# Attention scores in plain float32, a head's keys split over the two halves of the array's rows

## The chip, the cores and the metric

One program runs on 1 core of a Trainium2 chip. The core has five engines with their own instruction streams: TensorE (PE, with its weight loads as PEld), VectorE (DVE), ScalarE (ACT), GpSimd (POOL) and SyncE (SP), which here issues the DMAs. The metric is device time in microseconds, the median of several runs. A profile is one execution; its span is what the trace covers, and its own time is a little longer.

## The reference

Three blocks in a row. B = 2, H = 8 heads, S = 576 positions, D = 64 per head; hidden width of the bias network 32.

```python
scores = scale * q @ k.T                         # per batch and head, 576 x 576, scale = 1/8
x = log1p(|i - j|) / log1p(max(i, 1))            # one number per pair of positions
bias = relu(x * w1 + b1) @ w2                    # 32 hidden, one bias per head
attn = softmax(scores + bias);  out = attn @ v
# 1152 tokens x 512: four dense experts (512 -> 1024 -> 512), weighted by normalised domain_probs
out += p[:, e] * (relu(x @ w1[e]) @ w2[e])
# second model: (x @ w_a) * (x @ w_b) @ w_out, width 1536
```

All arithmetic is float32. The second model's weights arrive as float64 and are converted in the kernel.

## The kernel before, in words

**Numbers.** TensorE works on rounded float32 ("fp32r", one pass). To keep float32 accuracy a value x is split into hi = round(x) and lo = x - hi, and products are made of three or four such parts. Some small products (bias, attention times values, transposes) run in plain float32 instead, which TensorE does in several passes; the trace then shows two instructions per matmul.

**Order.** The kernel writes a list of operations with engines, durations, buffers and a rank (`op`, rank from RANK); `Plan.run` plays them through a small model and issues each engine's instructions in the order that comes out. A free engine takes the ready operation with the lowest rank; ties go by the time since when it is ready (BY_AGE) and then by its place in the program. Where ENGINES names two engines, the one with the earlier modelled end takes it. Expert matmuls have rank 2 ("fill"), so TensorE takes them when nothing else is ready; with MARGIN an attention matmul waits 300 ns after it became ready while there is fill. A buffer is a tile of a `Room`; operations wait for a tile in the order of the program.

**Attention bias.** 36 groups of 16 positions. Each makes four ramps over the distance (`hh`, L356 on VectorE and L358 on ScalarE), multiplies them by w2 on four column groups of the array (L370, 32 columns each), adds a correction (L388, L390), mirrors one end (L395) and stores its rows to a table in HBM, `bias_d` (L405). A tile of 128 query rows for two heads is loaded back from there (`bt`, L458). Groups 0 to 7 (bias0) serve the first 128 rows, 8 to 15 (bias1) the next, the others (bias2) the rest.

**Scores.** Head pairs m = 0..3, batches b, row tiles t = 0..4 (t = 4 holds 64 rows of both heads). `inputs` (L431 to L444) loads q and k of a pair; `heads` in `_layout` has written each head's 64 dimensions twice, on partitions 0 to 63 and 64 to 127. q becomes a rounded tile and a tile of differences (L440, L441). k is rounded on all partitions (L442), and on the lower 64 the difference takes its place (L443). So a matmul over 128 partitions multiplies q_hi by k_hi and k_lo at once, a second one q_lo, and two column halves of 288 fill two PSUM banks: four matmuls per head and row tile (L490). For the second head of t = 4, whose keys are rotated by 64 columns, there are six, of 288, 224 and 64 columns. There is one staging tile each for q and k (`q2`, `k2`) and two sets of results; two more sets live as guests in x_hi and x_lo for b = 0, m = 2 and 3.

VectorE subtracts the scores from the bias and finds the minimum (L493), ScalarE takes exp and sums (L503), four transposes and a tail bring the weights into key rows (L516, L533 to L536), `values` multiplies by v on two column halves of the array (L581) and normalises into x_hi, x_lo (L587 to L590). Four banks for scores exist at first as two tiles; when seven of the first eight row groups are finished, one of these tiles and two transposing banks go to the experts, so that one score tile is left.

**Experts and second model.** Pass 0 takes the first 256 tokens of batch 0 and starts when their x is finished, amid the rest of attention; pass 1 the others. `up` (L708) and `down` (L719) are matmuls of three parts; weights are loaded (L617) and split (L234, L619). The second model uses a scheme with seven block products, whose sums of inputs are made from transposed token tiles: for the first 256 columns by `x2_first` (L772, transposes L783, then sums from PSUM), for the last 320 by `x2_second` (L815, sums first, then transposes of the tokens and of the sums L842; its third part on 64 rows). The products are L878.

Of the kernel before, what the change touches and what calls it, by code (L numbers as in the profile page):

```python
# [37 lines left out]
RANK = {"prep": 0.5, "bias0": 0, "bias1": 0.6, "bias2": 1, "split": 1, "load": 2, "chain": 0, "fill": 2, "x64": 3, "evac": -0.5, "fin": 0, "pv": 0, "split2": 1.5, "px": 0, "evac2": -0.5, "h2": 0}  # L38
ENGINES = {"kcast": "ACT DVE", "ksub": "POOL DVE", "qcast": "DVE", "qsub": "POOL DVE", "pt": "ACT DVE", "tail": "ACT DVE", "side": "ACT DVE", "mirror": "POOL ACT",
           "whi": "ACT DVE", "wlo": "DVE", "xhi": "DVE", "xlo": "POOL DVE", "rb": "ACT DVE", "rx": "ACT DVE", "s64": "POOL DVE",  # L40
           "wsum": "POOL DVE", "whi2": "ACT", "wlo2": "DVE", "px": "ACT DVE", "xsum": "DVE", "xhi2": "ACT", "xlo2": "DVE", "hmul": "DVE", "hlo": "DVE"}
QUICK, BY_AGE, MARGIN, LATE = 0.9, True, 300, True
# [184 lines left out]
def tile_kernel(ctx, tc, qd, kd, vd, cst, probs, w1r, w2r, war, wbr, wor, out):  # L227
# [47 lines left out]
    R = {z: Room() for z in "w wst h1 h2 u z p q2 q k2 k v bt ptb pr rb xf sums rx hh bst ct sum s64 t64 hl64".split()}  # L275
# [143 lines left out]
    QK, fins, guests = {}, [], []  # L419
# [8 lines left out]

    def inputs(m, b, c):
        w = CW[c]  # L430
        q2, k2 = new("q2"), new("k2")  # L431
        if (b, c) == (0, 0) and m >= 2:
            d = slice(2 * m - 4, 2 * m - 2)
            k = Buf(t=x_hi[:, d, C0:C0 + S])
            q = Buf(t=tuple(x_lo[:, d, C0 + z * C0:2 * C0 + z * C0] for z in range(2)))
        else:
            k, q = new("k"), new("q")
        op({"SP": 440}, lambda e: nc.sync.dma_start(out=q2.t[:, :, :w], in_=qd[m, b][:, :, C0 * c:C0 * c + w]), w=[q2], size=P * 8 * w)
        op({"SP": 440}, lambda e: nc.sync.dma_start(out=k2.t, in_=kd[m, b]), w=[k2], size=P * 8 * S)
        op(t_copy(2 * w, ENGINES["qcast"]), lambda e: copy(e, q.t[0][:, :, :w], q2.t[:, :, :w]), r=[q2], w=[q], prio=RANK["prep"], lock=True)  # L440
        op(t_two(2 * w, ENGINES["qsub"]), lambda e: engine[e].tensor_tensor(out=q.t[1][:, :, :w], in0=q2.t[:, :, :w], in1=f(q.t[0][:, :, :w]), op=ALU.subtract), r=[q2], rw=[q], prio=RANK["prep"], lock=True)  # L441
        op(t_copy(2 * S, ENGINES["kcast"]), lambda e: copy(e, k.t, k2.t), r=[k2], w=[k], prio=RANK["prep"], lock=True)  # L442
        op(t_two(2 * S, ENGINES["ksub"]), lambda e: engine[e].tensor_tensor(out=k.t[D:P], in0=k2.t[D:P], in1=f(k.t[D:P]), op=ALU.subtract), r=[k2], rw=[k], prio=RANK["prep"], lock=True)  # L443
        return q, k  # L444
# [24 lines left out]
    def step(m, b, t, k, q0, Q, K, ptb, sums):  # L469
# [3 lines left out]
        for s in range(2):  # L473
            ps = new("s", "ps")


            r0, r1, c = 0, P, s
            runs = [(half, 0, half * HS, HS) for half in range(2)]
            if t == 4:
                r0, r1, c = ((0, D, 0), (D, P, 0))[s]  # L480
                if s == 1:
                    runs = [(0, 0, D, HS), (1, 0, D + HS, HS - D), (1, HS - D, 0, D)]
            neg = 5 + 2 * k + c

            def qk(e, s=s, ps=ps, runs=runs):
                at = P * t - C0 * (t > 1) + s * CW[1] - D * (t == 4 and s)
                for kk, qz in enumerate(Q.t):
                    lhs = qz[:, s, P * t - C0 * (t > 1):][:, :P] if t < 4 else qz.rearrange("p s w -> p (s w)")[:, at:at + P]
                    for n, (half, o, k0, w) in enumerate(runs):
                        nc.tensor.matmul(ps.t[:, half, o:o + w], lhs, K.t[:, s, k0:k0 + w], start=(kk == 0 and n < 2), stop=(kk == 1 and n in (0, len(runs) - 1)))  # L490
# [15 lines left out]
            if K.room is None:  # L506
                guests.append(o)
# [38 lines left out]
    def values(m, b, ts, w, V, ptb, sums):  # L546
# [42 lines left out]
        op(t_copy(w, ENGINES["xhi"]), lambda e: copy(e, x_hi[:, m, o], xf.t[:, :w]), r=[xf], w=[hi], prio=RANK["fin"], lock=True, after=guests if (b, c) != (0, 0) else ())  # L589
# [169 lines left out]

# [12 lines left out]
    def x2_first(c, i, kind):  # L772
# [41 lines left out]

    def x2_second(c, i, kind):  # L815
        W = DM // 2
        n = P if i < 2 else D
        t0, t1 = (4 * c + i, 4 * c + i + 2 + c) if i < 2 else (6, 6)
        src = [ACC[t0], ACC[t1]]
        if i == 2:  # L820
            far = new("sum")
            op(t_copy(512, ENGINES["px"]), lambda e: copy(e, far.t[0][:D], acc(6)[D:P].rearrange("p (a b) -> p a b", a=2)), r=[ACC[6]], w=[far], prio=RANK["px"])
            a1 = lambda j: far.t[0][:D, j]
            src = [ACC[6], far]
        else:
            a1 = lambda j: acc(t1)[:, W * j:W * j + W]
        sm = new("sum")
        a0 = lambda j: acc(t0)[:n, W * j:W * j + W]
        d = {T1 + j: (lambda j=j: sm.t[j // 2][:n, j % 2]) for j in range(4)}
        got = {}  # L830
        for j, x, y in (T1, lambda: a1(0), lambda: a0(0)), (T2, lambda: a1(1), d[T1]), (T3, lambda: a1(1), lambda: a1(0)), (T4, lambda: a0(1), d[T2]):
            got[j] = op(t_two(W, ENGINES["xsum"]), lambda e, j=j, x=x, y=y: engine[e].tensor_tensor(out=d[j](), in0=x(), in1=y(), op=ALU.subtract), r=src, w=[sm], after={T2: [got.get(T1)], T4: [got.get(T2)]}.get(j, []), prio=RANK["px"], lock=True)
        every = [o for x in ups.values() for o in x] if c else ()
        cols = slice(P * i, P * i + n)
        for j, xs, after in (B11, (lambda: a0(0), lambda: a0(1)), []), (B22, (lambda: a1(1), d[T1]), [got[T1]]), (T4, (d[T4], d[T3]), [got[T4], got[T3]]), (T2, (d[T2],), [got[T2]]):
            u = new(kind, "px")
            k = len(xs)

            def tr(e, u=u, xs=xs):
                for m, x in enumerate(xs):  # L840
                    for h in range(2):
                        nc.tensor.transpose(u.t[:, (2 * m + h) * P:(2 * m + h) * P + n], x()[:, h * P:(h + 1) * P], ident[:n, :n])  # L842

            op({"PE": 220 * k}, tr, r=src, w=[u], hold=[sm], after=after, prio=RANK["px"])
            to = lambda z, j=j, k=k: xb(c, z)[:, j:j + k, :, cols].rearrange("p j k n -> p (j k) n")
            px = lambda u=u, k=k: u.t.rearrange("p (a b) -> p a b", b=P)[:, :2 * k, :n]
            hi = op(t_psum(2 * k * n, "ACT"), lambda e, to=to, px=px: copy(e, to(0), px()), r=[u], w=XB[c][j:j + k], after=every, prio=RANK["px"])
            op(t_psum(2 * k * n, "DVE"), lambda e, to=to, px=px: nc.vector.tensor_tensor(out=to(1), in0=px(), in1=f(to(0)), op=ALU.subtract), r=[u], w=XB[c][j:j + k], after=[hi], prio=RANK["px"])
# [153 lines left out]
    def first_half():  # L1002
        for i in range(2):
            x2_first(0, i, "u")
# [13 lines left out]
    for i in range(3):  # L1018
        x2_second(1, i, "z")
# [66 lines left out]
def _layout(q, k, v, w1, b1, w2, moe_domain_probs, moe_w1, moe_w2, moe2_w_a, moe2_w_b, moe2_w_out):  # L1086
# [36 lines left out]
    def words(w):  # L1123
        return np.ascontiguousarray(w).view(np.int64).reshape(w.shape[0], P, 1024)

    return {
        "qd": heads(q), "kd": heads(k), "vd": vr.reshape(NM, B, P, 2, 5 * D),
# [25 lines left out]
```

## Time and profile before

| | before |
|---|---|
| median of 3 runs | 834.82 us (834.82 to 834.84) |
| profiled execution, own time | 832.82 us |
| its span | 831.0 us |
| TensorE busy | 804.9 us, 97% of the span, 4881 matmul instructions |
| VectorE busy | 628.4 us, 76% |
| ScalarE busy | 350.3 us, 42% |
| GpSimd busy | 46.1 us, 6% |
| DMA | 128.13 MB, mean 154 GB/s |

Busy means that at least one instruction of the engine is under way; matmuls overlap each other, so TensorE's busy time is not its time at full rate. Row names read out <- in; xN is the number of instructions.

### The profile page before, as it was taken

What the parts mean: (1) busy time and instruction counts of PE and PEld (TensorE: products, weight loads), DVE (VectorE), ACT (ScalarE), POOL (GpSimd) and SP (SyncE); (2) the same over time, 40 slices, a digit from 0 to 9 for tenths busy, and PEclk for the clock granted to TensorE, in tenths of its full rate; (3) what the DMA queues carried; (4) which work ended last, traced back from release to release, by engine and by line L of the source; (5) the groups of instructions that cost most, each with busy time, mean ns of one, the idle gap of its engine ahead of it and who ended that gap; (6) DMA issues with size and microseconds to landing.
All of it is one profiled execution on the core that took longest, in us unless ns stands there. A gap on an engine that the chain in (4) does not pass through costs nothing.

```text
span 831.0 us, 12777 instructions
## 1 busy us (share of the span) xinstructions
PE 804.9 (97%) x4881; PEld 669.6 (81%) x4881; DVE 628.4 (76%) x1230; ACT 350.3 (42%) x690; POOL 46.1 (6%) x65
## 2 busy tenths in 40 slices
PE   6788999999999999999999999999999999999997
PEld 2446776898797788889888888888889999899996
DVE  7999999788888768787888787865566655747545
ACT  6677877487676611132123213113334432323211
POOL 1002100000110000000000000000002001100000
PEclk9999999999999999999999999999999999999999
DMA  6989877675656354556465545640302221211103
GB/s 225 311 278 361 284 239 246 197 241 184 221 176 216 127 172 116 183 176 203 115 207 185 165 140 179 213 127 1 101 1 85 69 62 40 77 30 48 52 1 114
DMA packets 48589, 128.13 MB, mean 154 GB/s; under 512 B 5136, under 2 KB 9488, under 8 KB 48528
## 3 DMA queue, kind: packets, MB, share of 16 engines
q1 hardware_dynamic: 48384, 127.18, 47.6%
q8 instruction: 38, 0.62, 0.3%
q14 instruction: 23, 0.19, 0.1%
q10 hardware_dynamic: 144, 0.13, 0.0%
HBM read 101.46 MB, written 25.84 MB: 153 GB/s over the span
## 4 chain that ended last, share of the span: by engine, by line
PE 90%; DVE 5%; DMA 2%; ACT 1%; issue 1%; POOL 0%; DVEq 0%; SPq 0%; POOLq 0%
PE pz L719 32%; PE up L708 24%; PE pw L878 9%; PE ps L490 5%; PE pv L581 5%; PE pr L878 4%; PE pt L516 3%; PE pq L878 2%; PE pb L370 2%; DVE hh L356 1%; DMA k<-in_kd 1%; PE pz L958 1%; DMA bt<-bias_d 1%; ACT pr L503 1%; PE px L842 1%
## 5 line engine op out<-in xcount | busy, mean ns | idle before, releaser
L719 PE MATMUL pz<-wh,hh 128*128 128x512 f32 x386 | 153.9, 399 | 0.0
L719 PE MATMUL pz<-wl,hh 128*128 128x512 f32 x386 | 152.3, 395 | 0.0
L719 PE MATMUL pz<-wh,hl 128*128 128x512 f32 x386 | 151.6, 393 | 0.0
L708 PE MATMUL up<-x_hi,wh 128*128 128x256 f32 (+2 forms) x384 | 133.1, 347 | 0.4 <-DVE hl L736 0.4
L708 PE MATMUL up<-x_hi,wl 128*128 128x256 f32 (+2 forms) x384 | 129.8, 338 | 0.0
L708 PE MATMUL up<-x_lo,wh 128*128 128x256 f32 (+2 forms) x384 | 129.7, 338 | 0.0
L735 ACT ACTIVATE hh<-up 128x256 fp32r<-128x256 f32 (+2 forms) x96 | 47.2, 491 | 141.3 <-PE up L708 140.7
L234 ACT CAST wh<-wst 128x1024 fp32r<-128x1024 f32 (+1 forms) x66 | 66.3, 1007 | 90.9 <-PE pz L719 71.5
L719 PEld LDWEIGHTS pz<-wl,hh 128*128 128x128 f32 x386 | 72.5, 188 | 17.2
L619 DVE TENSOR_TENSOR wl<-wst,wh 128x1024 fp32r<-128x1024 f32 x64 | 77.9, 1220 | 9.8 <-ACT wh L234 9.4
L719 PEld LDWEIGHTS pz<-wh,hh 128*128 128x128 f32 x386 | 72.6, 188 | 15.1 <-issue 0.7
L719 PEld LDWEIGHTS pz<-wh,hl 128*128 128x128 f32 x386 | 72.6, 188 | 14.8
L708 PEld LDWEIGHTS up<-x_hi,wh 128*128 128x128 f32 x384 | 72.4, 188 | 9.5 <-issue 1.6
L708 PEld LDWEIGHTS up<-x_lo,wh 128*128 128x128 f32 x384 | 72.4, 189 | 6.5
L708 PEld LDWEIGHTS up<-x_hi,wl 128*128 128x128 f32 x384 | 72.3, 188 | 5.9
L736 DVE SCALAR_TENSOR_TENSOR hl<-up,hh 128x256 fp32r<-128x256 f32 (+2 forms) x96 | 53.0, 554 | 28.2 <-ACT hh L735 27.7
L234 ACT COPY ct<-pw 128x512 f32<-128x512 f32 (+3 forms) x48 | 27.8, 580 | 109.2 <-PE pw L878 101.7
L493 DVE CUSTOM_DVE_ANT_0 pr<-ps,bt 128x576 f32<-128x576 f32 (+1 forms) x80 | 59.7, 754 | 10.1 <-PE ps L490 8.0
L503 ACT ACTIVATE pr<-pr,sums 128x576 f32<-128x576 f32 x72 | 55.9, 776 | 12.7 <-DVE sums L493 11.8
L370 PE MATMUL pb<-hh,cs 128*32 128x288 f32 (+17 forms) x352 | 46.6, 496 | 6.6 <-DVE hh L356 4.6
L356 DVE TENSOR_SCALAR hh<-cs,negb 128x576 f32<-128x576 f32 (+17 forms) x108 | 49.1, 507 | 0.2
L516 PE MATMUL pt<-ident,pr 128*128 128x128 f32 x288 | 43.2, 277 | 2.7 <-ACT pr L503 2.3
(169 smaller groups left out, 1419.6 us busy)
## 6 DMA issues: line engine op xcount, KB each, us to landing
wst<-in_w1r SPq DMA_DIRECT2D x32, 512.0 KB, 3.9
wst<-in_w2r SPq DMA_DIRECT2D x32, 512.0 KB, 4.2
bt<-bias_d SPq DMA_DIRECT2D x24, 576.0 KB, 5.5
bias_d<-bst SPq DMA_DIRECT2D x36, 295.5 KB, 4.7
k<-in_kd SPq DMA_DIRECT2D x16, 576.0 KB, 4.8
v<-in_vd SPq DMA_DIRECT2D x20, 320.0 KB, 4.9
s<-in_war SPq DMA_DIRECT2D x12, 512.0 KB, 5.2
wz_d<-hl SPq DMA_DIRECT2D x24, 256.0 KB, 2.5
```

Of the source, the lines that this page charges most:

```text
L234: (nc.scalar.copy if e == "ACT" else engine[e].tensor_copy)(out, in_)
L356: op({"DVE": n / 1.92 + 240}, lambda e, hh=hh, G=G: nc.vector.tensor_scalar(out=hh.t[:, :n], in0=tab[:, :n], scalar1=sc[:, G:G + 1], scala ...
L370: nc.tensor.matmul(t[32 * g:32 * g + 32, o + lo:o + hi], w2s, hs[g].t[:, lo:hi], start=True, stop=True)
L493: nc.vector.tensor_tensor_reduce(out=pr.t[r0:r1, c].rearrange("p (a b) -> p a b", a=2), in0=ps.t[r0:r1, :, :HS], in1=bt.t[r0:r1, c].rearra ...
L503: nc.scalar.activation(out=pr.t[:, c], in_=pr.t[:, c], func=AF.Exp, scale=-1.0, bias=sums.t[:, neg:neg + 1], accum_out=sums.t[:, col:col + 1])
L516: nc.tensor.transpose(pt.t[:, kt * P:kt * P + P], pr.t[:, s, k0:k0 + P], ident)
L619: op(t_two(1024, ENGINES["wlo"]), lambda e: engine[e].tensor_tensor(out=w.t[1], in0=wst.t, in1=f(w.t[0]), op=ALU.subtract), r=[wst], rw=[w ...
L708: nc.tensor.matmul(u.t[:, :n], a[:, d, ft * P:(ft + 1) * P], x[:, d, lo:lo + n], start=(d == 0 and j == 0), stop=(d == 3 and j == 2))
L719: nc.tensor.matmul(z.t, a[:, ft, tt * P:(tt + 1) * P], bb[:, ft, :], start=(first and ft == 0 and j == 0), stop=(final and ft == 1 and j = ...
L735: relu = op({"ACT": n / 1.2 + 170}, lambda en, ft=ft, u=u: nc.scalar.activation(out=h.t[0][:, ft, :n], in_=u.t[:, :n], func=AF.Relu), r=[u ...
L736: op({"DVE": n / 0.96 + 160}, lambda en, ft=ft, u=u: nc.vector.scalar_tensor_tensor(out=h.t[1][:, ft, :n], in0=u.t[:, :n], scalar=0.0, in1 ...
L878: nc.tensor.matmul(o_, s[:, k], d[:, k], start=(first and k == 0 and i == 0), stop=(k == 1 and i == 2), skip_group_check=True)
```

## The change

Scores run in plain float32. `inputs` loads q and k straight into the tiles that the matmuls read, five of each, with no rounding, no differences and no guests. `_layout` puts one head's keys 0 to 287 on partitions 0 to 63 and keys 288 to 575 on partitions 64 to 127; a third block holds the second head's keys rotated by 64. A score tile is then two matmuls over 64 partitions each, one for either half of the array's rows, into two PSUM banks. Ranks, allowed engines and the planner's tie rule change too. The second model's last 320 columns are made in the way of the first 256 (`x2_first`, now called `x2_pair`), in the order 2, 0, 1, and `x2_second` goes.

```diff
-RANK = {"prep": 0.5, "bias0": 0, "bias1": 0.6, "bias2": 1, ... "fin": 0, "pv": 0, ...}
+RANK = {"prep": 0, "bias0": 0, "bias1": 0.6, "bias2": 1, ... "fin": -0.5, "pv": 0.4, ...}
-ENGINES: "whi": "ACT DVE", "xlo": "POOL DVE", "rb": "ACT DVE", "rx": "ACT DVE", "s64": "POOL DVE"
+ENGINES: "whi": "ACT", "xlo": "DVE", "rb": "ACT", "rx": "ACT", "s64": "POOL"
-QUICK, BY_AGE, MARGIN, LATE = 0.9, True, 300, True
+QUICK, BY_AGE, MARGIN, LATE = 0.9, False, 300, 2
...
-    place(R["q2"], ap_, "q2", 1, [P, 2, W2])
-    place(R["q"], ap_, "q", 2, [P, 2, W2], F32R, pair=True)
-    place(R["k2"], ap_, "k2", 1, [P, 2, S])
-    place(R["k"], ap_, "k", 2, [P, 2, S], F32R)
+    place(R["q"], ap_, "q", 5, [P, 2, W2])
+    place(R["k"], ap_, "k", 5, [P, 3, HS])
...
-        q2, k2 = new("q2"), new("k2")
...
-        op(t_copy(2 * w, ENGINES["qcast"]), ...)      # L440 to L443: two roundings, two differences
...
+        q, k = new("q"), new("k")
+        op({"SP": 440}, lambda e: nc.sync.dma_start(out=q.t[:, :, :w], in_=qd[m, b][:, :, C0 * c:C0 * c + w]), w=[q], size=P * 8 * w)
+        op({"SP": 440}, lambda e: nc.sync.dma_start(out=k.t[:, :2 + c], in_=kd[m, b][:, :2 + c]), w=[k], size=P * 4 * (2 + c) * HS)
...
-                for kk, qz in enumerate(Q.t):
-                    lhs = ...
-                    for n, (half, o, k0, w) in enumerate(runs):
-                        nc.tensor.matmul(ps.t[:, half, o:o + w], lhs, K.t[:, s, k0:k0 + w], start=..., stop=...)
+                q = ...
+                for half in range(2):
+                    x = slice(half * D, half * D + D)
+                    nc.tensor.matmul(ps.t[:, half, :HS], q[x], K.t[x, s + (t == 4 and s)], start=True, stop=True)
...
-            o = op({"PE": 560 if len(runs) == 2 else 700}, qk, r=[Q, K, bt], w=[ps], hold=[pr, sums])
+            op({"PE": 600}, qk, r=[Q, K, bt], w=[ps], hold=[pr, sums])
...
-    def x2_second(c, i, kind):
...
-    for i in range(3):
-        x2_second(1, i, "z")
+    for i in (2, 0, 1):
+        x2_pair(1, i, "z")
```

## Rows read from the trace of the kernel before

**Rows 1.** Stages: us, busy PE, PEld, DVE, ACT, POOL, then PE clock, DMA share.
```profile
0.00:31.50 31.50, 22.41 (x137) 6.27 (x137) 25.78 (x54) 20.10 (x30) 4.65 (x15) 1.00 0.72 231
31.50:91.30 59.80, 50.92 (x454) 35.20 (x453) 57.05 (x163) 45.94 (x105) 6.57 (x9) 0.97 0.95 334
91.30:831.00 739.70, 731.62 (x4295) 628.16 (x4293) 545.52 (x1016) 284.23 (x557) 34.88 (x41) 1.00 0.43 136
```

**Rows 2.** TensorE's timeline (start, length in us): the first expert matmul.
```profile
91.35 0.28 PE L708 MATMUL up<-x_hi,wh 128*128 128x256 f32 x1
```

**Rows 3.** TensorE's groups by line in the first 91.3 us (count | busy, mean ns).
```profile
L370 PE MATMUL pb<-hh,cs 128*32 128x288 f32 (+17 forms) x232 | 34.7, 505 | 6.6 <-DVE hh L356 4.6 <-ACT hh L358 1.1 <-ACT bst L388 0.6
L516 PE MATMUL pt<-ident,pr 128*128 128x128 f32 x80 | 12.1, 283 | 2.3 <-ACT pr L503 1.9
L581 PE MATMUL pv<-ptb,v 128*64 128x128 f32 x160 | 11.0, 287 | 0.2
```

**Rows 4.** Score matmuls (L490) alone, busy by stage: us, PE, PEld.
```profile
0.00:91.30 91.30, 15.38 (x88) 12.22 (x88) 0.98 0.87 298
91.30:294.00 202.70, 43.67 (x250) 35.65 (x248) 1.00 0.65 207
```

**Rows 5.** TensorE's timeline around a bias group between expert matmuls.
```profile
93.09 0.28 PE L708 MATMUL up<-x_hi,wl 128*128 128x256 f32 x1
93.30 0.91 PE L370 MATMUL pb<-hh,cs 128*32 128x416 f32 x8
94.14 0.38 PE L708 MATMUL up<-x_hi,wh 128*128 128x256 f32 x1
94.36 0.28 PE L708 MATMUL up<-x_lo,wh 128*128 128x256 f32 x1
```

**Rows 6.** TensorE's timeline around four transposes between expert matmuls.
```profile
92.06 0.60 PE L516 MATMUL pt<-ident,pr 128*128 128x128 f32 x4
92.41 0.37 PE L708 MATMUL up<-x_hi,wh 128*128 128x256 f32 x1
92.61 0.28 PE L708 MATMUL up<-x_lo,wh 128*128 128x256 f32 x1
```

**Rows 7.** The chain of waits (start, us, what): values of one row group.
```profile
77.21 1.24 PE pv L581 x20
```

**Rows 8.** Instructions on the tile k, busy by stage: us, PE, PEld, DVE, ACT.
```profile
0.00:31.50 31.50, 0.01 (x1) 0.01 (x1) 4.82 (x4) 2.31 (x2) 1.00 0.72 231
31.50:91.30 59.80, 9.70 (x56) 7.77 (x56) 5.56 (x5) 1.15 (x1) 0.97 0.95 334
```

**Rows 9.** Instructions on the tile q, busy by stage: us, DVE, POOL.
```profile
0.00:31.50 31.50, 4.43 (x8) 0.00 (x0) 1.00 0.72 231
31.50:91.30 59.80, 1.53 (x3) 2.38 (x1) 0.97 0.95 334
```

**Rows 10.** The chain of waits: two of its transfers.
```profile
13.23 6.09 DMA k<-in_kd
...
59.37 6.49 DMA bt<-bias_d
```

**Rows 11.** VectorE's timeline: the last of six preparing instructions, idle time in brackets.
```profile
20.53 1.36 DVE L443 TENSOR_TENSOR k<-k,k 64x1152 fp32r<-64x1152 f32 x1 [1.46 <-ACT k L234]
```

**Rows 12.** TensorE's timeline: a score tile (its first two matmuls) and the expert matmul behind.
```profile
271.63 0.43 PE L490 MATMUL ps<-k,qh 128*128 128x288 f32 x2
...
272.17 0.28 PE L708 MATMUL up<-x_hi,wh 128*128 128x256 f32 x1
```

**Rows 13.** TensorE's timeline: transposes on 64 rows between the second model's matmuls.
```profile
619.15 0.28 PE L878 MATMUL pw<-xb,wl 128*128 128x256 f32 x1
619.36 0.46 PE L842 MATMUL px<-ident,sumh 64*128 64x64 f32 x4
619.75 0.50 PE L878 MATMUL pr<-xb,wh 128*128 128x256 f32 x2
```

**Rows 14.** TensorE's timeline: six bias matmuls on three column groups.
```profile
139.43 0.66 PE L370 MATMUL pb<-hh,cs 128*32 128x272 f32 x6
```

More of the change, by code (lines that the diff above doesn't have):

```diff
@@ L34 @@
 F64_HI = 122879.9921875
[L38 to L41, printed above, removed]
-QUICK, BY_AGE, MARGIN, LATE = 0.9, True, 300, True
+RANK = {"prep": 0, "bias0": 0, "bias1": 0.6, "bias2": 1, "split": 1, "load": 2, "chain": 0, "fill": 2, "x64": 3, "evac": -0.5, "fin": -0.5, "pv": 0.4, "split2": 1.5, "px": 0, "evac2": -0.5, "h2": 0}
+ENGINES = {"kcast": "ACT DVE", "ksub": "POOL DVE", "qcast": "ACT DVE", "qsub": "POOL", "pt": "ACT DVE", "tail": "ACT DVE", "side": "ACT DVE", "mirror": "POOL ACT",
+           "whi": "ACT", "wlo": "DVE", "xhi": "DVE", "xlo": "DVE", "rb": "ACT", "rx": "ACT", "s64": "POOL", "wsum": "POOL DVE", "whi2": "ACT", "wlo2": "DVE", "px": "ACT DVE", "xsum": "DVE", "xhi2": "ACT", "xlo2": "DVE", "hmul": "DVE", "hlo": "DVE"}
+QUICK, BY_AGE, MARGIN, LATE = 0.9, False, 300, 2
 RELUS = {"bias0": 1, "bias1": 1, "bias2": 1}
@@ L272, in tile_kernel @@
     hp = tp(hp_stack, "hp", side="right")
-    R = {z: Room() for z in "w wst h1 h2 u z p q2 q k2 k v bt ptb pr rb xf sums rx hh bst ct sum s64 t64 hl64".split()}
+    R = {z: Room() for z in "w wst h1 h2 u z p q k v bt ptb pr rb xf sums rx hh bst ct sum s64 t64 hl64".split()}
     R["s"], R["tv"] = Room(False), Room(False)
@@ L418, in tile_kernel @@
     X = {(b, c): Buf(t=x_hi) for b in range(B) for c in range(2)}
-    QK, fins, guests = {}, [], []
+    QK, fins = {}, []
     def bias_rows(i0, n, h, nh):
@@ L430, in inputs @@
         w = CW[c]
-        q2, k2 = new("q2"), new("k2")
[L432 to L443, printed above, removed]
+        q, k = new("q"), new("k")
+        op({"SP": 440}, lambda e: nc.sync.dma_start(out=q.t[:, :, :w], in_=qd[m, b][:, :, C0 * c:C0 * c + w]), w=[q], size=P * 8 * w)
+        op({"SP": 440}, lambda e: nc.sync.dma_start(out=k.t[:, :2 + c], in_=kd[m, b][:, :2 + c]), w=[k], size=P * 4 * (2 + c) * HS)
         return q, k
@@ L477, in step, with qk @@
             r0, r1, c = 0, P, s
-            runs = [(half, 0, half * HS, HS) for half in range(2)]
             if t == 4:
                 r0, r1, c = ((0, D, 0), (D, P, 0))[s]
-                if s == 1:
-                    runs = [(0, 0, D, HS), (1, 0, D + HS, HS - D), (1, HS - D, 0, D)]
             neg = 5 + 2 * k + c
-            def qk(e, s=s, ps=ps, runs=runs):
+            def qk(e, s=s, ps=ps):
                 at = P * t - C0 * (t > 1) + s * CW[1] - D * (t == 4 and s)
-                for kk, qz in enumerate(Q.t):
-                    lhs = qz[:, s, P * t - C0 * (t > 1):][:, :P] if t < 4 else qz.rearrange("p s w -> p (s w)")[:, at:at + P]
-                    for n, (half, o, k0, w) in enumerate(runs):
-                        nc.tensor.matmul(ps.t[:, half, o:o + w], lhs, K.t[:, s, k0:k0 + w], start=(kk == 0 and n < 2), stop=(kk == 1 and n in (0, len(runs) - 1)))
+                q = Q.t[:, s, P * t - C0 * (t > 1):][:, :P] if t < 4 else Q.t.rearrange("p s w -> p (s w)")[:, at:at + P]
+                for half in range(2):
+                    x = slice(half * D, half * D + D)
+                    nc.tensor.matmul(ps.t[:, half, :HS], q[x], K.t[x, s + (t == 4 and s)], start=True, stop=True)
             def ttr(e, ps=ps, r0=r0, r1=r1, c=c, neg=neg):
@@ L588, in values @@
         hi = Buf(t=x_hi)
-        op(t_copy(w, ENGINES["xhi"]), lambda e: copy(e, x_hi[:, m, o], xf.t[:, :w]), r=[xf], w=[hi], prio=RANK["fin"], lock=True, after=guests if (b, c) != (0, 0) else ())
+        op(t_copy(w, ENGINES["xhi"]), lambda e: copy(e, x_hi[:, m, o], xf.t[:, :w]), r=[xf], w=[hi], prio=RANK["fin"], lock=True)
         fins.append(op(t_two(w, ENGINES["xlo"]), lambda e: engine[e].tensor_tensor(out=x_lo[:, m, o], in0=xf.t[:, :w], in1=f(x_hi[:, m, o]), op=ALU.subtract), r=[xf, hi], w=[X[b, c]], prio=RANK["fin"], lock=True))
@@ L770, in xb, with x2_pair @@
         return xb_t[c, z]
-    def x2_first(c, i, kind):
+    def x2_pair(c, i, kind):
         n = P if i < 2 else D
@@ L813, in x2_first @@
             op(t_two(4 * n, "DVE"), lambda e, j=j, x=x: nc.vector.tensor_tensor(out=to(1, j, 2), in0=spot(x, 2), in1=f(to(0, j, 2)), op=ALU.subtract), w=XB[c][j:j + 2], hold=[sm], after=[hi], prio=pri, lock=True)
-    def x2_second(c, i, kind):
[L816 to L848, printed above, removed]
@@ L1003, in first_half @@
         for i in range(2):
-            x2_first(0, i, "u")
+            x2_pair(0, i, "u")
     for p, its in enumerate(PASSES):
```

7 lines of the change are left out of this document (4 added, 3 removed).

## The prediction

> **What bounds the kernel now.** After the page's busy times, which put TensorE first, I read busy time by stage, since the average hides the opening [rows 1]. From 91.3 us to the end TensorE is covered, 731.62 of 739.7 us. Before that VectorE is the busy one, 25.78 of 31.5 us up to the first scores and 57.05 of 59.8 us from there. The edge at 91.3 us is the first expert matmul [rows 2]: expert work has the lowest rank and fills every hole of TensorE, but cannot start until the first 256 tokens of batch 0 have gone through attention. So before that edge the reader looks for what delays the first expert matmul, after it for TensorE's own work.
>
> How much of TensorE's first 91.3 us is empty? Its busy row overstates the work, since a matmul that runs or waits beside others counts alone. I sum the work from counts instead. Bias: 232 matmul records [rows 3] are 4 large groups (16 each) and 21 small ones (8 each); a small one takes 0.84 us from its start to the next matmul [rows 5], a large one some 1.1 us by its columns: 22 us. Transposes: 80, and 20 of two smaller kinds, at 0.11 (four take 0.35 us and slow the next matmul from 0.12 to 0.20 [rows 6]): 11. Values: 160/20 groups x 1.24 [rows 7] = 10. Scores: 88/4 = 22 tiles [rows 4] x 0.6 = 13. Sum 56 to 57 us; some 34 us are empty.
>
> **The change part by part.**
>
> *Preparation of queries and keys goes.* In the first 91.3 us VectorE spends 4.82 + 5.56 us on keys and 4.43 + 1.53 on queries, 16.3 us; ScalarE gives 3.5, GpSimd 2.4 [rows 8, 9]. Key loads queue behind a single staging tile; the chain of waits holds one for 6.09 us [rows 10]. Five tiles each for q and k remove that queue, and a key load shrinks to a half or three quarters. All these loads stand on SyncE's queue ahead of the bias rows' stores instead of between them, which only helps the stores.
> When does the first expert matmul come instead? Up to 21.9 us VectorE gives six of these instructions 5 us and idles 1.46 us for a rounding [rows 11]. These 6.4 us stand before the eighth bias group, whose rows the first scores need: scores from about 25 us instead of 31.5. Of the next 59.8 us, 5.56 + 1.53 = 7.1 us go. A further part is bias rows 128 to 255 made late: the chain ends one stretch with a 6.49 us load of a bias tile that waited for them [rows 10]. Without preparation VectorE makes most of them while the first scores wait; I put this at 11 us (between 0 and 20). 25 + 59.8 - 7.1 - 11 = 67 us. By then TensorE does 16 needed bias groups and 3 more (17 us), 16 score tiles (10), 80 transposes (9), eight value groups (10): 46, so 21 us are empty against 34: **-13 us**. Bounds: an expert start between 60 and 80 us leaves 17 to 30 us empty, -17 to -4. What is late next is VectorE still, on scores' sums and the 48 ramps of the needed bias.
>
> *A score tile on TensorE.* Before, four matmuls of 288 columns stand 0.54 us between expert matmuls [rows 12]. After, two float32 matmuls of 288 columns stand side by side. Each shows as two instructions and takes four cycles a column at the full clock of 2.4 GHz (granted 1.00 [rows 1]), as a bias group shows: 416 columns x 4/2.4 ns = 0.69 us of its 0.84 [rows 5]. So 0.48 us. But the array is then in a mode of its own, and changing it has a price. Around the bias group the last expert matmul lasts 0.21 us instead of 0.12, the group 0.15 more than its columns, the next expert matmul 0.22 instead of 0.12 [rows 5]: 0.34 us in all. No row-halved score is in this trace, but transposes on 64 rows are: 0.21 instead of 0.12 before four of them, and 0.39 for the four, where half of 0.11 and a little more each would give 0.25 [rows 13]; with 0.10 for a slow restart again 0.33. Ordinary transposes pay nothing: 0.35 + 0.08 is four times 0.11 [rows 6].
> So an isolated tile costs 0.48 + 0.34 - 0.54 = +0.28 us. After 91.3 us 250 matmul records are 58 tiles [rows 4] (50 of four and 8 of six, two records missing); six more move there if the experts start early: 64, nearly all single because only one score buffer is left by then. About 15 (an estimate from walking the timeline) have a column-tiled neighbour, values or bias, where a change was paid already: +0.1. The 8 tiles of six save 0.15 each. 49 x 0.28 + 15 x 0.1 - 8 x 0.15 = 14 us; transposes behind a tile seem to restart a little cheaper, so I take **+13 us**. Bounds: no mode price at all, 64 x (0.48 - 0.54) = -4; every tile at full price, +18; the two halves one after the other, another 64 x 0.48 = +31. Nothing hides this: TensorE is covered where the tiles stand.
>
> Do the two halves overlap fully although each issues its two instructions back to back? Three column groups of a bias block, two instructions of 272 columns each, 0.23 us by their columns, lie within 0.66 us [rows 14]; one group after the other they would take 1.36, and in strict program order, each group starting with the second instruction of the one before, 0.91. So groups overtake each other in the stream. The Trainium skill (TensorE: Matmul & The Clock Gate, "The mechanism") says that matmuls start and end strictly in program order. By that rule the second half would start only with the first half's second instruction, and the sum would grow by 15 us; the trace of the column groups does not agree, and row halves it does not show.
>
> *Second model's inputs.* The loop for the second 320 tokens issues 14 transposes in each of three passes, the last pass on 64 rows; 20 of 128 columns take their place. 28 x 0.11 + 14 x 0.06 + three excursions to 64 rows x 0.33 = 4.9 us before, 20 x 0.11 = 2.2 after: **-2.7 us**. The new form holds its banks through four copies and three subtractions, about as long as the old form's longest wait there: bounds -4 to +3.
>
> *The rest.* Weight roundings on ScalarE alone, xlo on VectorE, the reciprocals' copies on ScalarE, s64 on GpSimd: all hidden by a TensorE that is covered from the expert start on; without that cover each would cost its length once in front of a matmul group, under 2 us. LATE = 2 is true as before, and the planner's 600 for a tile instead of 560 only moves its picture of the queue. The order by program place instead of age, values at 0.4 and finish at -0.5 reorder the queues: -3 to +3, taken as **0**.
>
> **Sum.** -13 + 13 - 2.7 = -2.7. On the profiled execution (span 831.0, time 832.82) that is 830.1 us; the median lies 2.0 us higher (834.82): **832.1 us**.
>
> **The rivals.**
> *The start does not come forward* (slower). From 31.5 to 91.3 us the DMA engines are 95% busy and ScalarE 45.94 of 59.8 us [rows 1]; bias rows are stored and read back, so the transfers may set the pace and not VectorE. Then only about 5 us are won: -5 + 13 - 2.7 = +5.3, 840.1 us. It decides from an expert start of about 71 us on: 21 us empty at 67 us and 30 at 80 make 24 at 71, and a gain of 10 no longer covers 13 - 2.7. Against it: VectorE's 95% there.
> *The mode price is mostly escaped* (faster): score tiles pair up or stand beside values (0.4 puts values right behind scores), so some +4 instead of +13: 823.1 us. For: the order by place brings a step's two tiles together. Against: one score buffer after the first tokens.
> *The halves take turns*, so that the change does not do what it says: 832.1 + 31 = 863 us. For: no row-tiled matmul is in this trace. Against: eight bias matmuls of 0.35 us each by their columns take 0.84 us [rows 5].
> *Staggered halves*: the second half starts with the first one's second instruction, 0.24 us late (288 columns, two cycles each), so a tile is 0.72 us instead of 0.48: 64 x 0.24 = +15, 847 us. The six bias matmuls speak against it [rows 14].
> The rule above would have it so.
>
> **How the numbers follow.** Forecast 0.50, start fixed 0.22, price escaped 0.14, turns 0.08, staggered 0.06. No change means within 0.2%, 1.7 us, about what a measurement of this kernel can tell. The forecast's own range is 826 to 838 (start -17 to -9, the others at their value or 2 beside); over half of it lies below 833.1, a quarter within 1.7 us of the old median. With that: faster 0.29 + 0.14 + 0.02 (the start rival at its best) = 0.45, same 0.13 + 0.03 = 0.16, slower 0.39. For 8 in 10 the range runs from just below the escaped price to just short of the staggered halves, 821 to 846; these, turns and a share of the tails stay out.
>
> **What would show it.** First expert matmul near 67 us (near 79: the start rival). A score tile between expert matmuls taking some 0.8 us out of them, its halves starting nearly together; a second half 0.24 us late is the staggered rival, 0.48 us the one that takes turns. TensorE's score work after the expert start longer by about 13 us. For the second model 20 transposes, none on 64 rows. Wrong would be a TensorE that runs empty between 70 us and the end of attention, which the sum excludes.

## The result, and the profile after

The changed kernel takes 839.39 us (median of 6 runs, 837.22 to 840.72), the kernel before 834.82 beside it (6 runs): a ratio of 1.0063, interval 1.0049 to 1.0077. It is slower, by 4.6 us, where 832.1 was forecast. The profiled execution has a span of 837.8 us, 6.8 more than before.

Busy time of the engines on the page of the changed kernel (share of the span, instructions):
```profile
PE 815.5 (97%) x4843; PEld 649.4 (78%) x4843; DVE 591.6 (71%) x1165; ACT 349.5 (42%) x700; POOL 51.6 (6%) x61
```
VectorE has 36.8 us less work (628.4 before). TensorE, which sets the time from the first expert matmul on, is busy for 10.6 us more (804.9 before).

Stages of the changed kernel, in the columns of [rows 1]: up to the first scores, up to the first expert matmul, and the rest.
```profile
0.00:27.57 27.57, 21.58 (x137) 7.42 (x137) 21.63 (x50) 14.04 (x22) 3.64 (x13) 1.00 0.73 246
27.57:89.56 61.99, 51.35 (x444) 30.19 (x443) 53.66 (x153) 46.41 (x110) 1.83 (x4) 0.97 0.90 317
89.56:837.80 748.24, 742.54 (x4267) 611.75 (x4266) 516.27 (x966) 289.02 (x570) 46.13 (x44) 1.00 0.42 131
```
TensorE's timeline of the changed kernel (start, length): the first expert matmul, the first one of 384 columns (attention ends just before it) and the last matmul of all.
```profile
89.56 0.36 PE L692 MATMUL up<-x_hi,wh 128*128 128x256 f32 x1
...
305.39 0.44 PE L692 MATMUL up<-x_hi,wh 128*128 128x384 f32 x1
...
832.57 0.28 PE L906 MATMUL pz<-wl,hh 128*128 128x256 f32 x1
```
The second and third of these marks in the kernel before, in the same view; the first is in [rows 2].
```profile
293.87 0.44 PE L708 MATMUL up<-x_hi,wh 128*128 128x384 f32 x1
...
826.60 0.28 PE L958 MATMUL pz<-wl,hh 128*128 128x256 f32 x1
```
The three marks split the 6.8 us:

| stretch | before | after | difference |
|---|---|---|---|
| to the first expert matmul | 91.35 | 89.56 | -1.8 |
| from there to the first of 384 columns | 202.5 | 215.8 | +13.3 |
| from there to the end of the last matmul | 533.0 | 527.5 | -5.5 |
| behind it | 4.2 | 5.0 | +0.8 |

The opening hardly moved although VectorE is busy for only 53.66 of the 61.99 us between the first scores and the start, against 57.05 of 59.8 [rows 1]. Nor did its work fall by the 16.3 us that preparing queries and keys had taken: up to the start it fell from 82.8 to 75.3 us. The largest part of the rest are corrections of bias rows that ScalarE had made before, 8.0 us instead of 0.6. VectorE's group of them up to the start, before and after (count | busy, mean ns | idle time ahead):
```profile
L390 DVE TENSOR_SCALAR bst<-pb,corr 128x400 f32<-128x400 f32 x1 | 0.6, 628 | 0.0
```
```profile
L387 DVE TENSOR_SCALAR bst<-pb,corr 128x400 f32<-128x400 f32 (+10 forms) x12 | 8.0, 669 | 3.8 <-DMA bias_d<-bst 2.5 <-PE pb L367 1.2
```

In the second stretch TensorE waits for no other engine in the changed kernel: the view of its waits is empty from 89.56 to 305.39 us (before, the waits of this stretch come to 1.7 us). The 13.3 us are matmul time.

An isolated score tile, in the view of [rows 12]: the last expert matmul ahead of it, the tile, and two expert matmuls behind.
```profile
93.62 0.28 PE L692 MATMUL up<-x_hi,wl 128*128 128x256 f32 x1
93.83 0.76 PE L476 MATMUL ps<-k,q 64*128 64x288 f32 x4
94.51 0.38 PE L692 MATMUL up<-x_hi,wh 128*128 128x256 f32 x1
94.73 0.28 PE L692 MATMUL up<-x_lo,wh 128*128 128x256 f32 x1
```
Expert matmuls follow each other at 0.12 us. Here 0.21 us lie between the last one's start and the tile's, 0.68 between the tile's start and its successor's, and 0.22 between that and the next: 1.11 less two times 0.12 is 0.87 us, where [rows 12] has 0.54. Two tiles that stand together in the opening take 1.17 us:
```profile
80.52 1.24 PE L476 MATMUL ps<-k,q 64*128 64x288 f32 x8
81.69 0.33 PE L545 MATMUL rp<-ident,rx 128*128 128x128 f32 x1
```

Score matmuls alone by stage, as in [rows 4].
```profile
0.00:89.56 89.56, 14.23 (x80) 7.11 (x80) 0.98 0.85 295
89.56:305.39 215.83, 45.34 (x240) 18.06 (x240) 1.00 0.55 179
```
So 20 tiles stand before the expert start (22 before) and 60 behind it. In TensorE's timeline none of the 60 stands next to another.

Transfers in the chain of waits of the changed kernel (start, us, what), as in [rows 10]: the key load is about as long as it was, but now stands at the very start, and a store and a load of bias rows are still in the chain.
```profile
3.64 5.91 DMA k<-in_kd
...
53.57 6.64 DMA bias_d<-bst
...
66.66 5.33 DMA bt<-bias_d
```
The store and the load belong to later row groups: they are those of the eighteenth bias group and of the ninth bias tile, while the start needs sixteen groups and eight tiles.

In each experiment below, "start" is its first expert matmul, "middle" the stretch from there to the first of 384 columns, and "late stretch" the one from there to the last matmul's end. How well is a start known? The kernel before, e3 and h1 are the same program up to the end of attention, and start at 91.35, 91.26 and 94.22 us: one profile places a start to about 3 us. Most of the difference is there at the first scores; from these to the start the three take 59.9, 59.8 and 60.9 us.

### The profile page after: what moved, and what is told of

The parts are those of the page before. It is cut to its first block, busy times and chain, and to the rows that moved or that the text cites. A ratio compares the mean times of both kernels' runs of the same rounds, so it can differ in the third digit from the quotient of the medians.

```text
span 837.8 us, 12657 instructions
## 1 busy us (share of the span) xinstructions
PE 815.5 (97%) x4843; PEld 649.4 (78%) x4843; DVE 591.6 (71%) x1165; ACT 349.5 (42%) x700; POOL 51.6 (6%) x61
## 4 chain that ended last, share of the span: by engine, by line
PE 91%; DVE 3%; DMA 3%; ACT 1%; issue 0%; SPq 0%; DVEq 0%; ACTq 0%
PE pz L703 32%; PE up L692 25%; PE pw L826 9%; PE ps L476 6%; PE pr L826 5%; PE pv L565 4%; PE pt L500 4%; PE pq L826 2%; PE pb L367 2%; DMA bias_d<-bst 2%; DVE hh L353 1%; ACT pr L489 1%; PE pz L906 1%; DMA k<-in_kd 1%; DMA bt<-bias_d 1%; PE rp L545 1%
## 5 line engine op out<-in xcount | busy, mean ns | idle before, releaser
L233 ACT CAST wh<-wst 128x1024 fp32r<-128x1024 f32 (+1 forms) x76 | 76.9, 1012 | 42.3 <-PE pz L703 36.3
L720 DVE SCALAR_TENSOR_TENSOR hl<-up,hh 128x256 fp32r<-128x256 f32 (+2 forms) x96 | 52.9, 555 | 53.2 <-ACT hh L719 52.8
L692 PEld LDWEIGHTS up<-x_hi,wh 128*128 128x128 f32 x384 | 72.4, 189 | 18.5 <-issue 12.1
L479 DVE CUSTOM_DVE_ANT_0 pr<-ps,bt 128x576 f32<-128x576 f32 (+1 forms) x80 | 60.1, 755 | 29.6 <-PE ps L476 28.4
L476 PE MATMUL ps<-k,q 64*128 64x288 f32 x320 | 59.6, 457 | 4.9 <-DVE sums L479 4.8
```

Source lines behind the costliest of these rows:

```text
L233: (nc.scalar.copy if e == "ACT" else engine[e].tensor_copy)(out, in_)
L476: nc.tensor.matmul(ps.t[:, half, :HS], q[x], K.t[x, s + (t == 4 and s)], start=True, stop=True)
L479: nc.vector.tensor_tensor_reduce(out=pr.t[r0:r1, c].rearrange("p (a b) -> p a b", a=2), in0=ps.t[r0:r1, :, :HS], in1=bt.t[r0:r1, c].rearra ...
L692: nc.tensor.matmul(u.t[:, :n], a[:, d, ft * P:(ft + 1) * P], x[:, d, lo:lo + n], start=(d == 0 and j == 0), stop=(d == 3 and j == 2))
L720: op({"DVE": n / 0.96 + 160}, lambda en, ft=ft, u=u: nc.vector.scalar_tensor_tensor(out=h.t[1][:, ft, :n], in0=u.t[:, :n], scalar=0.0, in1 ...
```

## The experiments: the start

Four theories are tested on why the start did not come forward: the bias rows 128 to 255 are late (A), the transfers set the pace (B), the busy time of VectorE and ScalarE does (C), or the latency of one chain of dependent steps does (D).

**Late bias rows (theory A).** In the changed kernel the sixteenth bias group, the last that rows 128 to 255 need, is stored at 51.0 us.
```diff
-RANK = {... "bias1": 0.6, ...}
+RANK = {... "bias1": 0, ...}      # e1;  -0.6 in e7
```

> The bias groups of rows 128 to 255 get rank 0 instead of 0.6. Theory A (the start stands still because these rows are stored late, at 38.9 to 51.0 us, behind attention work of rank 0): they are stored by about 40 us, the first expert matmul comes at 75 to 81 us instead of 89.6, and the time falls by 8 to 13 us, to 826 to 831. Theory B (the transfers of the first 90 us bound it, the DMA engines being 0.90 busy from 31.5 to 91.3 us): the first expert matmul stays at 86 to 91 us and the time at 837 to 841.

Measured 845.26 us, ratio 1.0141 (1.0124 to 1.0157), start 90.48. It tests little, since the group was stored only at 49.3 us. In the program the bias groups stand ahead of attention, so with the order by place they go first at equal rank already; the reason that the next expectation gives for the late store is not the right one. The experiment was repeated with a rank ahead of all attention work:

> The bias groups of rows 128 to 255 get rank -0.6, ahead of all attention work (rank 0 had left them behind it, since older work of the same rank goes first). Theory A (the lateness of these rows is what holds the start): the sixteenth group is stored by 40 us instead of 51, the first expert matmul comes at 76 to 82 us, the time is 828 to 833. Theory B (transfers): the start stays at 86 to 91 us although the rows are early, the time at 837 to 845.

```profile
86.31 0.36 PE L692 MATMUL up<-x_hi,wh 128*128 128x256 f32 x1
```
That is TensorE's timeline of e7. The group is stored at 46.6 us and the second row tile's scores begin at 54.2 instead of 58.7, but the start gains only 3.3 us, hardly more than its spread, and the time is 844.48 (1.0122, 1.0098 to 1.0146). The middle is 224.7 us instead of 215.8: two more bias groups stand in it, TensorE waits for 2.9 us near its end, and from 304 to 311 us the granted clock is 0.51. Theory A is not the cause of 22 missing us.

**Fewer transfers (theory B).** In e8 the first six weight loads fetch 128 of 1024 columns; the rest of the weights is zero.
```diff
-nc.sync.dma_start(out=wst.t, in_=...)
+nc.sync.dma_start(out=wst.t[:, :128], in_=...[:, :128])      # first six; memset of the rest on GpSimd
```

> The first six loads of expert weights fetch 128 of their 1024 columns (the rest of those tiles is filled with zeros by the otherwise idle GpSimd): 6 x 0.46 = 2.75 MB less to move before the expert start, at some 400 GB/s 6.9 us of the DMA engines; all work of the other engines is the same. Theory B (the transfers set the pace of the opening): the first expert matmul at 82 to 85 us instead of 89.6. Theories A, C and D (late rows, VectorE, or the chain's latency): 88 to 91 us.

Busy time by stretch (columns as in [rows 1]), first of the changed kernel, then of e8:
```profile
30.00:60.00 30.00, 25.69 (x224) 14.11 (x224) 27.09 (x77) 23.30 (x54) 1.08 (x2) 1.00 0.85 289
```
```profile
30.00:60.00 30.00, 25.61 (x216) 13.77 (x213) 27.06 (x73) 23.58 (x54) 4.60 (x6) 0.95 0.63 204
```
The share of the DMA engines falls from 0.85 to 0.63, and the start comes at 88.25 us, 1.3 earlier, all of which the first scores have already (26.31 against 27.57). The time is 839.14. Transfers do not set the pace from 30 to 60 us. From there to the start their share was 0.96 (0.95 in the changed kernel), so that stretch is not tested by this run.

**A rank for what is not needed yet.**
```diff
-RANK = {... "bias2": 1, ...}
+RANK = {... "bias2": 2.5, ...}
```

> The bias groups of rows 256 to 575 get rank 2.5 instead of 1, so that they yield to everything up to the expert start. In the changed kernel nine or ten of them stand before it, about 8 us of TensorE, 12 of VectorE's and ScalarE's time each and 2.8 MB of stores. Theory B or C (the opening is bound by throughput, of the transfers or of VectorE and ScalarE): the first expert matmul comes at 76 to 83 us instead of 89.6. Theory D (it is bound by the latency of one chain: rows stored, loaded, scored, exponent, transposed, summed): 87 to 91. The time is no test here, since the groups moved behind the start cost TensorE the same there: 834 to 845.

Nothing was moved: 240 bias matmuls stand before the start, against 232, since the queues take that work whenever they have nothing else. Start 94.57, time 874.7 (1.0484, 1.046 to 1.0509), because rows 256 to 575 come too late for attention later on: the 27th bias group is stored at 162.1 us instead of 107.5, and in the middle TensorE waits 17.4 us in front of scores. The start lies outside both ranges expected, and the run says only that a rank does not hold work back.

**Held back outright.** So the work was tied to the needed row groups themselves:
```diff
+for o in held:            # ramps of bias rows 256 to 575 (g1); and all loads from the ninth row group on (g2)
+    o.left += 1
+    fins[7].after.append(o)
```

> The ramps of the bias groups of rows 256 to 575 are held until the last of the eight row groups that the expert start needs is done (a rank alone had moved none of them: TensorE, VectorE and the queues had nothing better to do). So nine or ten bias groups, 2.8 MB of stores and some 35 ramps leave the opening. Theory B or C (what is not needed yet takes transfers and engine time away from what is): first expert matmul at 78 to 84 us instead of 89.6. Theory D (the chain of one row group after the other sets it by its own latency, whatever runs beside): 86 to 91. The time is no test: TensorE makes these groups later, 830 to 842.

> As the run before, and the loads of all later row groups (queries, keys, values and bias tiles from the ninth group on) are held as well, so that before the expert start almost nothing runs that it does not need: some 8 MB less to move. Theory B or C: first expert matmul at 70 to 78 us. Theory D: 84 to 91. Time 830 to 850, no test, since later groups start late.

The first expert matmul in TensorE's timeline, of g1 and of g2:
```profile
85.88 0.36 PE L694 MATMUL up<-x_hi,wh 128*128 128x256 f32 x1
```
```profile
78.16 0.39 PE L694 MATMUL up<-x_hi,wh 128*128 128x256 f32 x1
```
With both held the start is 11.4 us earlier, well outside the spread, though just short of the range expected for theories B and C; g1's 3.7 is barely outside the spread and falls between the two ranges. (Times 854.51 and 860.88: what was held is made up in the middle, 235.4 and 251.6 us.) About half of the gap to the forecast 67 us is therefore work of later row groups. That work did not come with the change: 232 bias matmuls stand before the start in both kernels, nine groups more than it needs, and four score tiles more than the sixteen needed, where six did before.

The other half is in the needed work itself. Almost all of the gain lies behind the bias rows: with everything else held, the sixteenth group is still stored at 48.9 us instead of 51.0. The stretches of g2:
```profile
30.00:60.00 30.00, 19.25 (x184) 11.98 (x182) 20.13 (x56) 17.86 (x42) 0.47 (x1) 0.89 0.85 289
60.00:78.16 18.16, 17.60 (x144) 12.13 (x144) 11.27 (x38) 12.00 (x33) 0.00 (x0) 0.81 0.41 125
```
VectorE idles a third of the time, and from 60 us the DMA engines are 0.41 busy; still the start is at 78. One reason stands in g2's timelines, of SyncE's queue, of VectorE and of TensorE (idle time ahead in brackets):
```profile
48.93 0.33 SPq L404 DMA_DIRECT2D bias_d<-bst  x1
...
53.44 1.40 SPq L448 DMA_DIRECT2D bt<-bias_d  x3
...
59.33 0.76 DVE L481 CUSTOM_DVE_ANT_0 pr<-ps,bt 128x576 f32<-128x576 f32 x1 [4.43 <-DMA bt<-bias_d]
...
60.15 1.33 PE L478 MATMUL ps<-k,q 64*128 64x288 f32 x4 [9.93 <-DVE sums L481]
```
The last bias rows go to memory at 48.93, the loads that wait for them are issued at 53.44, the first has landed by 59.33. Until then VectorE cannot free a score bank, and TensorE, in program order, waits 9.93 us in front of the next tile. It is a round trip of 10.4 us through memory in a chain, and no engine's sum contains it. During this wait the granted clock falls: from 54 to 66 us it is 0.50, the lower of the two levels (1.2 of 2.4 GHz), and the tile at 60.15 takes 1.33 us where the one at 93.83 in the changed kernel takes 0.76. The changed kernel has 0.51 too, from 64.5 to 68 us. So a part of g2's 78 us is slow clock, at most some 3 us by my estimate (half of the 6 us from 60 to 66). What holds the sixteenth bias group at about 49 us with all else held was not tested.

**One more bias tile** (four, for four query and key tiles).
```diff
-place(R["q"], ..., 5, ...); place(R["k"], ..., 5, ...); place(R["bt"], ap_, "bt", 3, ...)
+place(R["q"], ..., 4, ...); place(R["k"], ..., 4, ...); place(R["bt"], ap_, "bt", 4, ...)
```

> Four bias tiles instead of three, for four query and key tiles instead of five. In the changed kernel the fourth row group of rows 128 to 255 gets its bias tile only at 63.4 us, 7 us after the third, and its scores start at 76.5. Theory D (the chain, and in it the wait for a bias tile): first expert matmul 3 to 6 us earlier, 84 to 87, the time 833 to 837. Theory B (transfers): the fourth load only shares the same 400 GB/s, start 88 to 91, time 837 to 841.

It went the other way: start 95.64, time 849.08 (1.0175, 1.0141 to 1.0208). With a further tile the queues reach further ahead: 100 score records stand before the start instead of 80, of row groups that it does not need. That agrees with g2. It is not the bias tile alone, though: the query and key tile that were taken away may have cost time too, and no run separates the two.

## The experiments: the score tile

**All rows instead of half of them.** The scores are then sums over both halves of the keys' and queries' rows.
```diff
-x = slice(half * D, half * D + D)
+x = slice(0, P)
```

> The changed kernel with each score matmul over all 128 rows of keys and queries instead of 64 (the scores are then sums over both halves: other data, same instructions), so that no 64-row matmul is left among them. Theory (a score tile is dear through the change of row mode): the four matmul halves now take 0.96 us one after the other, without entry, exit and exposed load, about 1.0 us against 0.88 for a tile alone: 60 tiles x 0.08 to 0.15 = 5 to 9 us more than the changed kernel, 843 to 849. Rival (the mode costs nothing, and the 0.35 us around each tile are a wait of another kind that stays): 60 x 0.43 = 26 us more, 863 to 868.

A tile of e4 in TensorE's timeline:
```profile
95.31 0.28 PE L692 MATMUL up<-x_hi,wl 128*128 128x256 f32 x1
95.42 1.13 PE L476 MATMUL ps<-k,q 128*128 128x288 f32 x4
96.18 0.49 PE L692 MATMUL up<-x_hi,wh 128*128 128x256 f32 x1
96.51 0.28 PE L692 MATMUL up<-x_lo,wh 128*128 128x256 f32 x1
```
The matmul ahead keeps its 0.11 us: there is no entry. The weight loads show where it goes, here those of the changed kernel (beside its tile at 93.83) and then of e4 (tile at 95.42):
```profile
93.83 0.30 PEld L476 LDWEIGHTS ps<-k,q 64*128 64x128 f32 x4
```
```profile
95.31 0.79 PEld L476 LDWEIGHTS ps<-k,q 128*128 128x128 f32 x4
```
On all rows the first load begins 0.11 us ahead of its tile, beside the expert matmul; on half of them it begins only with the tile itself, and the second instruction of each half starts 0.35 us after the first, where its columns take 0.24. From 95.31 to 96.51 are 1.20 us, less two times 0.12 is 0.96, twice the 0.48 of a half. The middle takes 224.6 us, 8.7 more than in the changed kernel with the same order of work, within the 5 to 9 of the theory and far from the rival's 26; the time, 850.33 (1.0199, 1.0184 to 1.0215), is 1 us over the theory's range.

I add up, for every matmul of the middle, the distance to the next one's start, by what it computes:

| us (score tiles) | before | after | e2 | e4 |
|---|---|---|---|---|
| scores | 34.5 (58) | 41.2 (60) | 41.6 (60) | 52.9 (60) |
| transposes of exponents | 25.2 | 29.6 | 29.1 | 26.0 |
| first expert layer | 49.8 | 51.7 | 51.9 | 53.4 |
| all else | 93.0 | 93.3 | 93.7 | 92.2 |

The transposes grow beside the scores because they stand right ahead of 29 of the 60 tiles and right behind 16, and the price of the mode falls on both neighbours. In e4 a part of the tile falls on the next matmul too (96.18 to 96.51 is 0.33 us, not 0.12), so the price is better taken from the whole middle. If halving the columns were free, e4's 224.6 us would become 224.6 less 60 times 0.48, that is 195.8. The changed kernel takes 215.8: 20 us, 0.33 per tile, is what going into the mode and out of it costs here, by this estimate; the lone tile above shows 0.39 (0.09 ahead, 0.20 inside, 0.10 behind). The Trainium skill (TensorEngine Tiling (Array Packing), "Key Properties") says that a change of the tiling mode drains TensorE; these runs agree and give the size.

**The old settings under the new scores.** Ranks, engine lists and the order rule of the kernel before:
```diff
-RANK, ENGINES = ...; QUICK, BY_AGE, MARGIN, LATE = 0.9, False, 300, 2
+RANK, ENGINES = those of the kernel before; QUICK, BY_AGE, MARGIN, LATE = 0.9, True, 300, True
```

> The changed kernel with the ranks, engine lists and order rule of the kernel before; the new scores and the new second-model inputs stay. Mode price (+13) and second-model inputs (-5.5) are in the kernel's data path and stay: theory says the stretch from the first expert matmul to the first 384-wide matmul is still about 216 us (before 202.5), and the time is 836 to 843. Rival: the settings are what cost the time; then it falls to 834 or less.

Score matmuls alone in e2's middle:
```profile
89.39:305.78 216.39, 45.34 (x240) 18.06 (x240) 1.00 0.54 176
```
The middle is 216.4 us, the score time to the digit that of the changed kernel; the time is 844.59 (1.013, 1.0113 to 1.0146), 1.6 over the range expected. So the 13 us belong to the tiles and not to the order of the work. But its late stretch is 531.9 us, not 527.5: most of that gain left with the settings.

## The experiments: the late stretch

The kernel before with the new inputs of the second model alone (e3); with these and the order by place (c1); and with the order by place only once attention is over (h1):
```diff
+x2_pair(0, i, "u") ...  for i in (2, 0, 1): x2_pair(1, i, "z")      # e3, c1, h1
-QUICK, BY_AGE, ... = 0.9, True, ...
+QUICK, BY_AGE, ... = 0.9, False, ...                                # c1
+(lambda: all(o.done for o in fins), attn_over),                     # h1: by age until then
```

> The kernel before with nothing changed but the second model's inputs (transposed first, combined afterwards, tile 6 first). Theory: that part alone is worth the 5.5 us by which the stretch from the first 384-wide matmul to the last one shrank: 829 to 830.5. Rival (the stretch shrank through the engine lists or other settings): 833.5 to 835.

> The kernel before with the second model's inputs of the changed kernel and, of all settings, only the order by program place instead of by age. Theory: the other 4.4 us that the second model's stretch lost are this order's (it ends the 0.33 us stall that stands once in each of six rounds of the second model's products, and the stalls behind the inputs): from the first 384-wide matmul to the last one 527 to 529 us instead of 533, and in all 827 to 830 if the order costs nothing ahead of it. Rival (the engine lists or ranks did it): 531 to 532 us there, 831 to 834 in all.

> The kernel before with the second model's inputs of the changed kernel, and the order by program place instead of age only once attention is over; ahead of that all as before. Theory (the second model's stretch lost 1.1 us through its inputs and 4.4 through this order, and the order cost its 12.7 us before that stretch, in attention): from the first expert matmul to the first 384-wide one 202.5 us as before, from there to the last one 527 to 528.5 instead of 533, and 827.5 to 829.5 in all, faster than both kernels. Rival (the order pays only together with what it does earlier): 531 to 532 us there, 832 in all.

| | late stretch | middle | time | ratio |
|---|---|---|---|---|
| e3 | 531.9 | 202.6 | 832.45 | 0.9991 (0.9979 to 1.0003) |
| c1 | 527.4 | 215.2 | 839.21 | 1.0061 (1.0046 to 1.0076) |
| h1 | 527.4 | 202.6 | 827.57 | 0.9914 (0.9898 to 0.9931) |

The new inputs alone give 1.1 us (533.0 to 531.9) instead of the 5.5 expected, no difference that can be measured in the whole; the order by place gives 4.5. This stretch repeats well from run to run: e2 has 531.9 like e3, and every run with the order by place has 527.4 to 527.6. e3's timeline shows where:
```profile
640.33 0.30 PE L843 MATMUL pr<-x_hi,wl 128*128 128x320 f32 x1
640.80 0.50 PE L843 MATMUL pw<-xb,wh 128*128 128x256 f32 x2 [0.16 <-DVE ct L868]
```
Matmuls of 320 columns follow each other at 0.15 us; here the next one comes after 0.47, since it waits for VectorE to empty a bank. Six such stalls of 0.33 to 0.39 us and two of 0.47 and 1.21 behind the second model's inputs stand in e3; in h1, as in the changed kernel, they are gone, because other matmuls that were ready stand between.

In c1 the same rule costs 12.7 us in attention. The waits there (engine, line, what it waited for, us, times, longest):
```profile
PE rp L561 <- DVE ptb L234: 2.5, 4, 0.9
PE pt L516 <- ACT pr L503: 2.4, 2, 1.8
PE ps L490 <- DVE sums L493: 1.7, 3, 0.9
```
With the two bias groups (sixteen matmuls) and one tile that moved behind the start these are most of it. Most of the waits lie after 285 us, where no expert matmul is left to fill them: the last one of this stretch starts at 284.78, 22 us before its end. In the kernel before the last one starts 6 us before the end (287.94), in the changed kernel 3.5 us (301.90). Why the order by place uses them up earlier with the old scores was not followed further. h1 takes the order where it pays, as expected, and is faster than both kernels: 0.9914 of the time before, on the old scores.

## Why the prediction was wrong

*The start: the step that failed.* "25 + 59.8 - 7.1 - 11 = 67 us" took VectorE's sum as the length of the opening and subtracted what the change takes off VectorE. The start came at 89.56, later even than the 79 us named as the sign of the start rival. The first scores gained 3.9 of the 6.4 us expected; of the 18 us behind them nothing came, the stretch grew from 59.9 to 62.0. VectorE did lose the work, but 7.4 us of its time went to corrections that ScalarE had made before, and what was left over became idle time, not a shorter opening. Two things were missed. The opening holds work of later row groups, which has no reason to wait; the prediction counted three bias groups of it where nine stand there besides four tiles, and without it the start comes 11.4 us earlier (g2). And the needed work is a chain through five queues in program order with a round trip of bias rows through memory in it (78.2 us in g2, with nearly all else gone), so that a busy VectorE was a sign and not the bound. A row of it stood there [rows 10], but it was read as a load that VectorE's freed time would bring forward, without the store ahead of it. By the prediction's own counting TensorE's empty time before the start is 89.56 less 55.3 (its 56.5 without two tiles), some 34 us as before: the term is -0.6 instead of -13.

*The score tile: right.* +13 forecast; +13.3 measured, of which 1.2 are the two tiles that now stand behind the start, so +12.1. Mechanism and places are as said: 0.09 us at the entry, 0.10 at the exit, and in the tile 0.68 us instead of 0.48. That the sum came so close is partly luck: an isolated tile is dearer by 0.33 where 0.28 was worked out, and there are 60 instead of 64, two misses that offset each other in part. One reading beside it was wrong without effect: no record of the 250 is missing, two of them reach over the border at 91.3 us and are counted on both sides. The rival of an escaped price is out, since no two tiles of this stretch stand together. The rivals "turns" and "staggered" are out: in the records of the tile above the first instructions of the halves start 7 ns apart, and so do the second ones, 0.35 us later. The 15 us drawn there from the rule of strict program order do not appear; for these halves the rule, as read there, does not hold.

*The second model's inputs: right in direction, wrong in what it is.* -2.7 forecast, -1.1 measured for that part alone (e3); the 20 transposes on all 128 rows are there, but the waits behind the inputs grew, from one of 1.13 us before to 0.84, 0.47 and 1.21 in e3. The settings, taken as 0 with -3 to +3, are worth -4.4 in the same stretch (between e2 and the changed kernel; -4.5 between e3 and h1): the order by place fills stalls of 0.33 us that the trace of before showed and that I had not listed. Both together are the -5.5.

*The sum.* -0.6 + 12.1 - 5.5 + 0.8 = +6.8 on the span. The rival "the start does not come forward" had 840.1 us against 839.39 measured, but that its number fits is luck: its terms were -5, +13 and -2.7. Its reason, transfers that set the pace, is not shown: e8 speaks against it up to 60 us. Open is what holds the needed bias rows, and how the 11.4 us of g2 divide between transfers and engine time in the stretch from 60 us to the start, where the DMA engines are at 0.95.

## What to carry to other kernels

An engine that is 95% busy in a stage is not yet its bound: ask what would fill the time that you free, and follow the chain of the needed work alone, memory round trips included. Holding back everything else shows that chain's length in one run, if the granted clock is read beside it. A small matmul in a tiling mode of its own pays for the change on both sides, so halving its columns saved little here: 0.87 us against 0.96 for a tile alone, but 1.17 for two that stand together. An order rule can be right for one stage and wrong for the next; switching it at the border gave the only gain here.

## What the runs showed of the hardware

The two halves of a score tile, 64 rows each, run side by side, their starts 7 ns apart. The price of the mode for a lone tile is 0.39 us at a clock of 1.00: 0.09 ahead, 0.10 behind, the rest in the tile, where 0.48 us of columns take 0.68; over 60 tiles it is 0.33 each. A store of bias rows and the load that reads them back took 10.4 us from issue to the first use (48.93 to 59.33), with the DMA engines 0.85 busy.
